# v three tiles ahead of k, and two LN1 transposes moved from TensorE to DMA, in a fused linear-attention and GEGLU kernel

## The chip, the cores and the metric

The kernel runs on one core of one Trainium2 chip. Its time is the device time of one execution in microseconds (us); the figure to compare is the median over several runs. One execution was also recorded by the hardware profiler, and every span, wait and duration below comes from that trace. The engines are named as the profile names them: PE is TensorE (with PEld, its weight loads), DVE is VectorE, ACT is ScalarE, POOL is GpSimd, and SP is SyncE, which here only issues DMAs. Each engine executes its own list of instructions in order and meets the others at semaphores.

## The reference

One sequence of S = 2048 rows with D = 640 columns, in bf16, goes through two blocks, both with a residual connection:

```python
def A(x):                       # H = 32 heads of Dh = 20
    qkv = (x @ wqkv) -> q, k, v per head
    pq, pk = q @ w_phi[h], k @ w_phi[h]
    phi_q = concat(softmax(pq), softmax(-pq))     # over the 20 features, so 40 per head
    phi_k = concat(softmax(pk), softmax(-pk))
    kv, z = phi_k^T v, sum over rows of phi_k     # per head: 40 x 20, and 40
    o = (phi_q @ kv) / (phi_q @ z + 1e-6)
    return o @ wo
def B(x):
    return (gelu(x @ w_gate) * (x @ w_up)) @ w_down     # F = 1536
h  = x + A(layernorm(x))
h2 = h + B(layernorm(h))
```

The attention is linear: all of kv must be summed over all rows before any row of o can be made.

## The kernel before

The rows are held as 16 tiles of 128 rows (x_sb, four tiles to a block). What matters here is the first phase, in which every row tile is normalized (LN1), transposed into LN1T, and multiplied by W_v and by a folded W_k.

*Order of work.* The program is written under a manual schedule: each engine executes its instructions in the order in which the Python code emits them. So the code's order is the queue order of every engine, SyncE's DMA queue included.

*Start.* Rows of x and W_v are loaded (lines 183 to 192); W_k is loaded transposed by five DMA transposes (`load_T`, L197). Meanwhile `warm` (L220) runs matmuls on constants. Tiles 0 and 1 are centred only and transposed on TensorE; their scale is applied later, when v and k are read out of PSUM.

*Fold.* `fold` (L224) multiplies the transposed W_k by a block-diagonal form of w_phi (BD), so that k and its feature map take one product, `Wk2`. It goes in five row chunks d = 0 to 4 of 128 rows: six matmuls each into a PSUM tile `wa`, and then one copy (cast) into Wk2, on ScalarE for the d in KA and on VectorE for the others (L249, L251).

*LN1.* `ln_st` emits the statistics of a tile: `bn_stats` and `bn_aggr` on VectorE (L116, L120), then on GpSimd the root (`ve`, `rstd`, L134 and L135), and, where ScalarE applies the norm, `mr` (L140). `ln_ap` applies it, on VectorE (`ln_dve`, L151) or on ScalarE (`ln_act`, L146). The result is transposed into LN1T either by TensorE (five transposes into PSUM, L159, and a copy out, L160) or by a DMA transpose issued by SyncE (L162). Before the change, tiles 2 to 5 go over TensorE and tiles 6 to 15 by DMA.

*v and k.* `v_mm` and `k_tile` are ten matmuls of 128x320 each (L287): five chunks c of LN1T by two halves u. `v_ev` copies v out of PSUM to vS on ScalarE (L307). `k_tile` goes on with two exponentials on ScalarE, of +k and -k (L320), which gives E.

*The passes.* The loop `for t in range(NT)` (L465) has 16 passes. Pass t emits, in this order: LN1 of tile t+6 on ScalarE (L470, from t = 1 on; in pass 4 later in the pass); `k_tile(t)`; in some passes a fold of W_q (FQ) or the products k^T v of finished tiles (`kv_tile`, in the passes that KVG names); `v_mm(t + 4)` and `v_ev(t + 4)`; statistics of later tiles (ST); `k_norm(t)`, which sums E per head on VectorE (L327), takes the reciprocal (L331) and scales v to `vt` on GpSimd and VectorE (L335); and DMA transposes of W_q. So v runs four tiles ahead of k. Tiles 0 to 4 of v are made before the loop.

*PSUM.* In this phase all products go through one pool, `psG`, of four buffers with two banks each (`gtile`, L106). A buffer is free for its next user when the engine that reads it has finished: for v after `v_ev`, for k after both exponentials.

*Later.* At the end of the loop the first q products, their exponentials and the last k^T v follow, W_g, W_u and W_d are loaded (L518, L533 to L536, each behind a small GpSimd copy that holds the load back), and the attention output, second LayerNorm and the GEGLU block are woven together (L688 to L829). `attn_a` (L580) reads the products of phi_q and kv out of PSUM in two copies, one for each half u.

Of the kernel before, what the change touches and what calls it, by code (L numbers as in the profile page):

```python
# [17 lines left out]
def kernel(  # L18
# [12 lines left out]
    nc = tc.nc  # L31
    P = 128
# [5 lines left out]
    NT = S // P  # L38
    NB = NT // 4
    NC = D // P  # L40
# [6 lines left out]
    VP = (0, 2, 4, 6, 9, 11, 12)  # L47
    KA, QA = (0, 1, 2, 4), (0, 1, 2, 3, 4)
    LQ = (7, 8, 9, 9, 10)
# [5 lines left out]

    KVG = {5: (0, 1), 9: (2, 3, 4, 5), 13: (6, 7, 8, 9)}
    KVQ = {0: (10, 11, 12)}
# [48 lines left out]
    def gtile(name):  # L106
        return psG.tile([P, 2, 512], F32, name=name, tag="G")
# [110 lines left out]
    def warm(*cols):  # L218
        for n in cols:
            nc.tensor.matmul(wu[:, 0, 0:n], lhsT=ones[:, 0:P], rhs=ones[:, 0:n], start=True, stop=True)  # L220

    warm(*[512] * 5, 256, *[P] * 14)

# [60 lines left out]

    def proj(ps, t, W, us=(0, 1), rows=False):
        for u, c in sorted(((u, c) for u in us for c in range(NC)), key=lambda x: x[::-1] if rows else x):
            nc.tensor.matmul(ps[:, u, 0:HD], lhsT=lnT(t, c), rhs=W[:, c, u * HD:(u + 1) * HD],  # L287
                             start=(c == 0), stop=(c == NC - 1))
# [3 lines left out]
    def v_mm(t, us=(0, 1)):  # L292
        if 0 in us:
            pv[t] = gtile("pv")
        proj(pv[t], t, Wv, us)
# [15 lines left out]
    def v_tile(t):  # L311
        v_mm(t)
        v_ev(t)

    def k_tile(t):
        pk = gtile("pk")
        proj(pk, t, Wk2, rows=t == 0)
        Ek[t] = ev.tile([P, 2, D], BF16, name="E", bufs=8)
        for s in range(2):
            nc.scalar.activation(Ek[t][:, s, :].rearrange("p (u f) -> p u f", u=2), pk[:, :, 0:HD],  # L320
                                 ACTF.Exp, scale=((lnp[t][2], nrstd[t]) if t in CT else (1.0, -1.0))[s])
# [121 lines left out]
    nc.sync.dma_start(x_sb[1][:, 2:4, :], x_v[:, 6:8, :])  # L443
    nc.sync.dma_start(x_sb[2], x_v[:, 8:12, :])
    nc.sync.dma_start(x_sb[3], x_v[:, 12:16, :])
    fold(WkT, Wk2, False, (0,))
    v_ev(2)
    fold(WkT, Wk2, False, (1,))
    v_mm(3)
    v_ev(3)  # L450
    ln_st(5, act=False, between=lambda: ln_ap(4, on_pe=True))
    fold(WkT, Wk2, False, (2,))
    ln_tp(4, True)
    fold(WkT, Wk2, False, (3, 4))
    v_mm(4)
    ln_ap(5, on_pe=True)
    v_ev(4)
    ln_tp(5)
    ln_st(6)
# [5 lines left out]
    for t in range(NT):  # L465
# [12 lines left out]
        for j in range(len(QT)):  # L478
            if t == QT[j]:
                q_mm(j)  # L480
                q_exp(j)
                for i in KVQ.get(j, ()):
                    kv_tile(i)
        if 0 < t < NT - 4:
            v_mm(t + 4)
        if late:
            ln_ap(t + 6, on_act=True)
        if 0 < t < NT - 4:
            v_ev(t + 4)
        for i in ST.get(t, ()):  # L490
# [26 lines left out]
    nc.gpsimd.tensor_copy(Wg[:, 0, 0:1], Eq[q - 2][:, 0, 1, 0:1])  # L517
    nc.sync.dma_start(Wg, wg_v)  # L518
    for t in range(13, NT):
# [11 lines left out]
    def load_late(j):  # L531

        nc.gpsimd.tensor_copy(Wu[:, 0, 0:1], Eq[j][:, 0, 1, 0:1])  # L533
        nc.sync.dma_start(Wu, wu_v)
        for f in (0, NF // 2):
            nc.sync.dma_start(Wd[:, f:f + NF // 2], wd_v[:, f:f + NF // 2])  # L536

# [42 lines left out]
    def attn_a(t, dve=0):  # L580
        attn_a_mm(t)
        AB, ab = ABs[t % 2], st[t, "ab"]
        for u in ((1, 0) if t in (4,) else (0, 1)):
            (nc.vector.tensor_copy if u >= 2 - dve else nc.scalar.copy)(
                AB[:, :, u * UH:(u + 1) * UH].rearrange("p s (r h) f -> p r s (h f)", r=2),
                ab[u][:, :, 0:2 * QH * KC].rearrange("p r (s x) -> p r s x", s=2))
        st[t] = AB
# [273 lines left out]
```

## Time and profile before

| | us |
|---|---|
| runs shown: median (lowest to highest of 3) | 275.06 (274.69 to 275.68) |
| the profiled execution | 274.73 |
| its span in the trace | 273.0 |
| first matmul of v starts | 6.63 |
| W_k folds and v of tiles 3 and 4 | 11.27 to 16.24 |
| k of tile 0 starts | 16.52 |
| k of tile 3 starts | 23.31 |
| first k^T v | 30.19 |

In the rows of a timeline the first number is the start of a piece of work from the start of the span, the second its length, then engine, line, operation, tiles written and read, shape, and how many instructions were merged. In brackets stands the idle time of the engine just before it and what ended that. TensorE's matmuls overlap at their ends, so the cost of a piece is best read from its start to the start of the next one. A line of the waits has who waited for whom, the total in us, how often, and the longest. The row PEclk has the granted TensorE clock in tenths in 40 equal slices of the span.

### The profile page before, as it was taken

How to read it: one execution, taken by the hardware profiler on the slowest of the kernel's cores; microseconds unless marked ns; L12 is line 12 of the kernel's file. 1: busy time of each engine (PE TensorE's matmuls, PEld its weight loads, DVE VectorE, ACT ScalarE, POOL GpSimd, SP SyncE). 2: the span in 40 equal slices, each digit the busy share in tenths (PEclk: the TensorE clock that was granted, in tenths of full speed). 3: DMA queues.
4: the chain of work that ended last, by engine and by line, in shares of the span. 5: the costliest groups of instructions: out<-in, count | busy, mean ns of one | idle time of the engine just before them, and what ended most of it. 6: DMA issues, size and time to landing. Idle time of an engine off the chain costs nothing.

```text
span 273.0 us, 7260 instructions
## 1 busy us (share of the span) xinstructions
PE 269.2 (99%) x3000; PEld 172.8 (63%) x3000; DVE 174.0 (64%) x331; ACT 140.4 (51%) x241; POOL 101.4 (37%) x221
## 2 busy tenths in 40 slices
PE   8999999999999999999999999999999999999996
PEld 5777777765555887788755455675555576444574
DVE  5889999996675866685457974346778333333332
ACT  5779996887799765364624256213345600223100
POOL 4248988786101226374213464102156400000000
PEclk9999999999999999999999999999999999999999
DMA  7972666351698022323202124110222211000011
GB/s 193 210 252 51 73 77 101 69 114 38 229 361 280 4 50 50 75 59 66 48 26 52 24 51 71 48 50 2 50 48 50 49 48 50 24 0 0 2 48 48
DMA packets 42400, 21.46 MB, mean 79 GB/s; under 512 B 35200, under 2 KB 40576, under 8 KB 42368
## 3 DMA queue, kind: packets, MB, share of 16 engines
q1 hardware_dynamic: 41712, 20.98, 31.7%
q8 instruction: 23, 0.38, 0.6%
q10 hardware_dynamic: 656, 0.03, 0.2%
q14 instruction: 9, 0.07, 0.1%
HBM read 10.18 MB, written 2.62 MB: 47 GB/s over the span
## 4 chain that ended last, share of the span: by engine, by line
PE 95%; DMA 2%; ACT 1%; DVE 1%; SPq 0%; issue 0%
PE gu L697 38%; PE pd L716 19%; PE pq L376 8%; PE po L637 8%; PE pk L287 8%; PE pv L287 7%; PE ab L565 2%; PE kvp L354 2%; DMA Wv<-in_A_wqkv_dram 2%; PE wa L240 1%; PE tp L159 1%; PE pv L303 1%; ACT vS L307 1%; DVE LN1T L160 0%; SPq L187 0%
## 5 line engine op out<-in xcount | busy, mean ns | idle before, releaser
L700 ACT ACTIVATE g<-gu 128x512 bf16<-128x512 f32 (+1 forms) x60 | 30.6, 511 | 63.4 <-PE gu L697 62.5
L703 DVE TENSOR_TENSOR GT<-gu,g 128x512 bf16<-128x512 f32 (+1 forms) x60 | 34.3, 578 | 43.8 <-PE gu L697 31.1
L697 PE MATMUL gu<-LN2T,Wg 128*128 128x512 bf16 (+1 forms) x300 | 61.8, 337 | 0.0
L697 PE MATMUL gu<-LN2T,Wu 128*128 128x512 bf16 (+1 forms) x300 | 61.7, 336 | 0.0
L716 PE MATMUL pd<-Wd,GT 128*128 128x320 bf16 (+2 forms) x396 | 53.5, 295 | 0.0
L716 PEld LDWEIGHTS <-GT 128*128 128x128 bf16 x396 | 37.9, 98 | 14.6 <-DVE GT L703 0.2
L697 PEld LDWEIGHTS <-Wu 128*128 128x128 bf16 x300 | 29.4, 98 | 22.6
L697 PEld LDWEIGHTS <-Wg 128*128 128x128 bf16 x300 | 28.6, 98 | 20.3
L287 PEld LDWEIGHTS <-LN1T 128*128 128x128 bf16 x290 | 27.8, 98 | 10.5
L335 POOL TENSOR_TENSOR vt<-vS,rs 128x672 bf16<-128x672 bf16 x23 | 31.0, 1371 | 5.9 <-DVE rs L331 4.0
L719 DVE TENSOR_TENSOR y<-pd,x_sb 128x320 bf16<-128x320 f32 (+2 forms) x29 | 13.9, 481 | 29.4 <-PE pd L716 29.4
L637 PE MATMUL po<-Wo,oT 128*128 128x320 bf16 x160 | 24.4, 299 | 0.0
L287 PE MATMUL pk<-Wk,LN1T 128*128 128x320 bf16 x160 | 24.2, 299 | 0.0
L376 PE MATMUL pq<-LN1T,Wq 128*128 128x512 bf16 x100 | 23.3, 379 | 0.0
L327 DVE TENSOR_REDUCE sk<-E 128x64 f32<-128x1280 bf16 x16 | 22.9, 1433 | 0.0
L381 ACT ACTIVATE Eq<-pq 128x1024 bf16<-128x1024 f32 (+1 forms) x26 | 20.0, 828 | 3.3 <-PE pq L376 3.3
L146 ACT ACTIVATE ln<-x_sb,v,rstd 128x640 bf16<-128x640 bf16 x14 | 12.9, 920 | 14.3 <-POOL v L676 14.2
L637 PEld LDWEIGHTS <-oT 128*128 128x128 bf16 x160 | 15.5, 98 | 7.0 <-ACT oT L160 0.5
L287 PE MATMUL pv<-Wv,LN1T 128*128 128x320 bf16 x130 | 19.8, 299 | 0.0
L320 ACT ACTIVATE E<-pk 128x640 bf16<-128x640 f32 x28 | 18.3, 716 | 2.2 <-PE pk L287 2.2
L614 DVE TENSOR_TENSOR tt<-AB,w 128x1280 bf16<-128x1280 f32 x12 | 17.8, 1487 | 1.0 <-POOL w L607 0.9
L594 POOL TENSOR_TENSOR pr<-AB 128x64 f32<-128x64 f32 x10 | 6.8, 678 | 28.1 <-DVE AB L575 20.7
(115 smaller groups left out, 295.6 us busy)
## 6 DMA issues: line engine op xcount, KB each, us to landing
out_dram<-y SPq DMA_DIRECT2D x15, 160.0 KB, 1.8
Wg<-in_B_w_gate_dram SPq DMA_DIRECT2D x1, 1920.0 KB, 8.8
Wu<-in_B_w_up_dram SPq DMA_DIRECT2D x1, 1920.0 KB, 8.9
Wd<-in_B_w_down_dram SPq DMA_DIRECT2D x2, 960.0 KB, 12.2
x_sb<-in_A_x_dram SPq DMA_DIRECT2D x2, 640.0 KB, 6.2
Wo<-in_A_wo_dram SPq DMA_DIRECT2D x1, 800.0 KB, 5.0
x_sb<-in_A_x_dram SPq DMA_DIRECT2D x4, 160.0 KB, 2.8
Wv<-in_A_wqkv_dram SPq DMA_DIRECT2D x2, 320.0 KB, 4.6
```

Of the source, the lines that this page charges most:

```text
L287: nc.tensor.matmul(ps[:, u, 0:HD], lhsT=lnT(t, c), rhs=W[:, c, u * HD:(u + 1) * HD], start=(c == 0), stop=(c == NC - 1))
L320: nc.scalar.activation(Ek[t][:, s, :].rearrange("p (u f) -> p u f", u=2), pk[:, :, 0:HD], ACTF.Exp, scale=((lnp[t][2], nrstd[t]) if t in C ...
L327: nc.vector.reduce_sum(sk, Ek[t].rearrange("p s (h f) -> p (s h) f", f=Dh), axis=AX.X)
L335: eng.tensor_tensor(vt[:, s], vS[t % 8], rs[:, s * H:(s + 1) * H, None].to_broadcast([P, H, VC]), ALU.mult)
L376: nc.tensor.matmul(pqs[j][:, i, :], lhsT=Wq2[:, kc, c * P:(c + 1) * P], rhs=LN1T[b][:, kc, :], start=(kc == 0), stop=(kc == NC - 1))
L381: nc.scalar.activation(Eq[j][:, :, s, :], pqs[j][:, 0:len(QG[j])], ACTF.Exp, scale=(1.0, -1.0)[s])
L614: nc.vector.tensor_tensor(tt.rearrange("p s (h f) -> p s h f", f=Dh), num, w[:, :, :, None].to_broadcast([P, 2, H, Dh]), ALU.mult)
L637: nc.tensor.matmul(pos[u], lhsT=st[t][:, c, :], rhs=Wo[:, c, u * HD:(u + 1) * HD], start=(c == 0), stop=(c == NC - 1))
L697: nc.tensor.matmul(gu[i][:, 0:n], lhsT=W[:, c, f * P:(f + 1) * P], rhs=LN2T[b][:, c, a0:a1], start=(c == 0), stop=(c == NC - 1))
L700: nc.scalar.activation(g[:, 0:n], gu[0][:, 0:n], ACTF.Gelu_apprx_tanh)
L703: nc.vector.tensor_tensor(st[b, "g", f][:, a0:a1], gu[1][:, 0:n], g[:, 0:n], ALU.mult)
L716: nc.tensor.matmul(ps, lhsT=st[b, "g", f][:, tl * P:(tl + 1) * P], rhs=Wd[:, f, f0:f1], start=(f == 0), stop=(f == NF - 1))
```

## The change

- The loop makes v three tiles ahead of k, `v_mm(t + 3)`, and tile 4 of v moves from before the loop into pass 1. The first k^T v (tiles 0 and 1) moves from pass 5 to pass 6.
- LN1 of tiles 4 and 5 is transposed by DMA, as that of the later tiles is; the TensorE transposes and the copies out of PSUM for them are gone.
- Before the loop the folds stand in another order, and k of tiles 0 and 1 is begun there by row chunks of W_k: chunks 0 to 2 of tile 0 and chunk 0 of tile 1 before the last fold, chunks 1 to 3 of tile 1 and 3 of tile 0 after it. `k_tile` adds the last chunk. The fold of chunk 2 is copied out by VectorE in place of ScalarE.
- The load of x_sb 2 is cut in two; its second half and x_sb 3 are issued after the DMA transposes of tiles 4 and 5.
- The loads of W_g and W_u are cut in three each, that of W_d in three in place of two.
- The warm-up matmuls have other sizes, with the same columns in all. In `attn_a`, tile 2 in place of tile 4 has its second half copied first.

```diff
-    KA, QA = (0, 1, 2, 4), (0, 1, 2, 3, 4)
+    KA, QA = (0, 1, 4), (0, 1, 2, 3, 4)
-    KVG = {5: (0, 1), 9: (2, 3, 4, 5), 13: (6, 7, 8, 9)}
+    KVG = {6: (0, 1), 9: (2, 3, 4, 5), 13: (6, 7, 8, 9)}
-    warm(*[512] * 5, 256, *[P] * 14)
+    warm(*[512] * 2, *[P] * 28)
-    def proj(ps, t, W, us=(0, 1), rows=False):
-        for u, c in sorted(((u, c) for u in us for c in range(NC)), key=lambda x: x[::-1] if rows else x):
+    def proj(ps, t, W, us=(0, 1), cs=None):
+        order = [(u, c) for u in us for c in range(NC)] if cs is None else [(u, c) for c in cs for u in us]
+        for u, c in order:
+    pks = {}
+
+    def k_part(t, *cs):
+        if 0 in cs:
+            pks[t] = gtile("pk")
+        proj(pks[t], t, Wk2, cs=cs)
+
     def k_tile(t):
-        pk = gtile("pk")
-        proj(pk, t, Wk2, rows=t == 0)
+        if t in pks:
+            pk = pks[t]
+            k_part(t, NC - 1)
+        else:
+            pk = gtile("pk")
+            proj(pk, t, Wk2)
...
     nc.sync.dma_start(x_sb[1][:, 2:4, :], x_v[:, 6:8, :])
-    nc.sync.dma_start(x_sb[2], x_v[:, 8:12, :])
-    nc.sync.dma_start(x_sb[3], x_v[:, 12:16, :])
+    nc.sync.dma_start(x_sb[2][:, 0:2, :], x_v[:, 8:10, :])
     fold(WkT, Wk2, False, (0,))
     v_ev(2)
     fold(WkT, Wk2, False, (1,))
+    ln_st(5, act=False, between=lambda: ln_ap(4))
+    fold(WkT, Wk2, False, (2,))
     v_mm(3)
     v_ev(3)
-    ln_st(5, act=False, between=lambda: ln_ap(4, on_pe=True))
-    fold(WkT, Wk2, False, (2,))
-    ln_tp(4, True)
-    fold(WkT, Wk2, False, (3, 4))
-    v_mm(4)
-    ln_ap(5, on_pe=True)
-    v_ev(4)
-    ln_tp(5)
+    fold(WkT, Wk2, False, (3,))
+    k_part(0, 0, 1, 2)
+    k_part(1, 0)
+    fold(WkT, Wk2, False, (4,))
+    k_part(1, 1, 2)
+    k_part(0, 3)
+    k_part(1, 3)
+    ln_ap(5)
+    nc.sync.dma_start(x_sb[2][:, 2:4, :], x_v[:, 10:12, :])
+    nc.sync.dma_start(x_sb[3], x_v[:, 12:16, :])
     ln_st(6)
     ln_st(7)
...
-        if 0 < t < NT - 4:
-            v_mm(t + 4)
+        if 0 < t < NT - 3:
+            v_mm(t + 3)
         if late:
             ln_ap(t + 6, on_act=True)
-        if 0 < t < NT - 4:
-            v_ev(t + 4)
+        if 0 < t < NT - 3:
+            v_ev(t + 3)
...
-    nc.sync.dma_start(Wg, wg_v)
+    for a, b in ((0, 2), (2, 4), (4, NC)):
+        nc.sync.dma_start(Wg[:, a:b], wg_v[:, a:b])
...
-        nc.sync.dma_start(Wu, wu_v)
-        for f in (0, NF // 2):
-            nc.sync.dma_start(Wd[:, f:f + NF // 2], wd_v[:, f:f + NF // 2])
+        for a, b in ((0, 2), (2, 4), (4, NC)):
+            nc.sync.dma_start(Wu[:, a:b], wu_v[:, a:b])
+        for f in range(0, NF, 4):
+            nc.sync.dma_start(Wd[:, f:f + 4], wd_v[:, f:f + 4])
...
-        for u in ((1, 0) if t in (4,) else (0, 1)):
+        for u in ((1, 0) if t == 2 else (0, 1)):
```

## The prediction

> **What bounds the kernel now.** I read the page's busy shares first, then what TensorE waits for, then its timeline, then ScalarE's, GpSimd's and SyncE's beside it.
>
> ```profile
> PE 269.2 (99%) x3000; PEld 172.8 (63%) x3000; DVE 174.0 (64%) x331; ACT 140.4 (51%) x241; POOL 101.4 (37%) x221
> PEclk9999999999999999999999999999999999999999
> ```
>
> ```profile
> PE wu L220 <- PEq L845: 0.8, 1, 0.8
> PE pv L303 <- DMA Wv<-in_A_wqkv_dram: 0.2, 1, 0.2
> ```
>
> TensorE is busy 99% of 273.0 us at the full granted clock, and its whole list of waits is two lines, both before 6.7 us. "Busy" alone proves little, because matmul ends are modelled; but ten 128x320 matmuls start 1.36 us apart in the whole first half (23.31 to 24.67, say), so there is no hidden idle time. What can be won is work that TensorE no longer does, or the little it loses between 6.6 and 17 us. The TensorE timeline there:
>
> ```profile
> 13.53 0.48 PE L240 MATMUL wa<-BD,WkT 128*128 128x140 bf16 x6
> 13.84 0.44 PE L159 MATMUL tp<-ident,ln 128*128 128x128 bf16 x5
> 14.12 0.84 PE L240 MATMUL wa<-BD,WkT 128*128 128x140 bf16 x12
> 14.87 1.53 PE L287 MATMUL pv<-Wv,LN1T 128*128 128x320 bf16 x10
> 16.24 0.44 PE L159 MATMUL tp<-ident,ln 128*128 128x128 bf16 x5
> 16.52 2.88 PE L287 MATMUL pk<-Wk,LN1T 128*128 128x320 bf16 x20
> ```
>
> Read start to start: five transposes cost 0.28 us (13.84 to 14.12, 16.24 to 16.52), one fold 0.31 (13.53 to 13.84), two folds 0.75 (14.12 to 14.87), so about 0.13 us there is waiting.
>
> ScalarE in the same stretch, then VectorE and GpSimd, which feed it:
>
> ```profile
> 18.08 0.79 ACT L320 ACTIVATE E<-pk,rstdc 128x640 bf16<-128x640 f32 x1 [0.35 <-PE pk L287]
> 18.77 0.79 ACT L320 ACTIVATE E<-pk,nrstd 128x640 bf16<-128x640 f32 x1
> 19.82 0.92 ACT L146 ACTIVATE ln<-x_sb,mr,rstd 128x640 bf16<-128x640 bf16 x1 [0.26 <-POOL mr L140]
> 20.65 0.77 ACT L320 ACTIVATE E<-pk,va 128x640 bf16<-128x640 f32 x1
> 21.32 0.78 ACT L320 ACTIVATE E<-pk,nrstd 128x640 bf16<-128x640 f32 x1
> ```
> ```profile
> 15.46 0.44 DVE L151 TENSOR_SCALAR ln<-x_sb,mv,rstd 128x640 bf16<-128x640 bf16 x1
> 15.81 0.88 DVE L116 BATCH_NORM_STATS2 stats<-x_sb 128x6 f32<-128x320 bf16 x2
> ```
> ```profile
> 18.05 0.43 POOL L140 TENSOR_SCALAR mr<-mv,rstd 128x1 f32<-128x1 f32 x1
> 19.52 0.26 POOL L140 TENSOR_SCALAR mr<-mv,rstd 128x1 f32<-128x1 f32 x1
> ```
>
> The line with 0.26 carries the forecast. ScalarE's LN1 of tile 7 stands ahead of the exponentials of k of tile 1, and already waits for a small GpSimd result that is ready at 19.78. That result comes 3.97 us after VectorE starts the statistics of tile 6 at 15.81, through a serial run of GpSimd instructions that waits for nothing on TensorE.
>
> SyncE issues all transfers in program order, each taking its time there:
>
> ```profile
> 11.65 0.58 SPq L443 DMA_DIRECT2D x_sb<-in_A_x_dram  x1
> 12.28 0.42 SPq L444 DMA_DIRECT2D x_sb<-in_A_x_dram  x1
> 18.46 19.69 SPq L162 DMA_TRANSPOSE LN1T<-ln  x8
> ```
>
> Whatever is put between the second and the third line moves the loads or the transposes behind it.
>
> **The change, part by part.**
>
> *Transposes of tiles 4 and 5.* TensorE loses two groups of 0.28 = 0.56 us. Their copies out of PSUM go too (0.49 on VectorE, 0.69 on ScalarE). The fold evacuation of W_k rows 2 moves from ScalarE (0.70) to VectorE (0.81): VectorE gets 0.32 us more and stood idle 0.19 and 0.69 us just there (before 12.55 and 14.32), so it is hidden; without that cover it would cost 0.32. ScalarE gets 1.4 us less.
>
> *Order to pass 3.* Folds 0 and 1 as before (to 12.17), fold 2 to 12.48, v of tile 3 to 13.9, fold 3 to 14.2, then k parts, fold 4 and k parts. The casts that these wait for end before they are needed: rows 2 on VectorE about 14.4 (wanted 14.7), rows 3 about 15.1 (wanted 16.1), rows 4 on ScalarE about 16.4 (wanted 16.7). So the 0.13 of waiting goes, some 0.04 comes back before v of tile 3, and TensorE is 0.65 us ahead: k of tile 0 ends at 16.96, k of tile 1 at 17.23, v of tile 4 at 18.59. k of tile 3, which started at 23.31 with one more v tile (1.36) done before it, is wanted at 23.31 - 1.36 - 0.65 = 21.30.
>
> *What is late next.* Four double-bank PSUM buffers serve k and v. When k of tile 3 wants one, k1, v4, k2 and v5 hold them, and the first free is that of k1, after both its exponentials. ScalarE reaches those only after LN1 of tile 7, and that only after GpSimd's result. In the new order VectorE starts the statistics of tile 6 no sooner than its own queue allows (about 15.42, after LN1 of tile 5) and no sooner than its rows land (issued at 11.65, 4.0 us to landing: 15.65). So the chain moves forward by 0.13 to 0.39 us, not by 0.65: the exponentials of tile 1, which ended at 21.32 + 0.78 = 22.10, end between 21.71 and 21.97, and k of tile 3 starts 0.04 later. TensorE waits 0.45 to 0.71 us there. With the v tile added back, 21.75 + 1.36 and 22.01 + 1.36 against 23.31: -0.20 to +0.06 us. I take -0.07, the middle, since the landing is the measured bound but less traffic follows behind it. The saving is nearly all given back.
>
> *After pass 3.* ScalarE's pass takes 2.57 us (22.00, 24.57 and 27.13 start its copies of v), TensorE's 2.72, so ScalarE is not late again. VectorE's chain from 20 us on is the same instructions in the same order, and does not hear of TensorE's lead. The first k^T v (tiles 0 and 1) took 0.88 at 30.19, against 1.45/2 = 0.73 each pair at 54.68; in pass 6, at about 31.5, its operands (VectorE's last at 29.87) are long ready: between 0 and 0.15 won, I take 0.10. The second, in pass 9, comes 1.4 us earlier than before (near 40.6), and its tile 5 needs a VectorE product that ends at 41.3; three tiles at 0.42 come first, to 41.9: no cost. By pass 13 all the moved v tiles are made up.
>
> *DMAs.* On SyncE the transpose of tile 4 issues at about 13.05 behind three row loads instead of being TensorE work; issue to landing of such transposes is 2.6 us in an empty queue (the median from 17 us on) and up to 5.1 (the W_k transposes in the full one): 15.7 to 18.2. It is wanted at 17.23, and the wait at k of tile 3 hides it until about 17.7. I take 16.5, as the queue empties by then. Tile 5 (issue 15.55, wanted 19.95) has more room. The rest of x_sb 2 and x_sb 3 goes from 12.28/12.75 to about 16.8/17.25; with the slowest such load (6.8) that is 24.05, and VectorE reads them from 24.13 on: nothing, but the margin is thin. SyncE's five more issues for W_g, W_u and W_d (0.4 each) delay the last by 2 us; W_u landed at 74.78 + 8.9 = 83.7 and is read from 89.7: nothing; SyncE's next transpose is past 94.
>
> *The rest.* The warm-up matmuls keep 4,608 columns, and at 0.107 us per 128 end where they did (4.83); what follows waits for VectorE's operand and then for W_v, landed at 6.6: nothing either way. The order of the two copies of tiles 2 and 4 out of PSUM changes which buffer comes free first, by one copy (0.75 on ScalarE, 0.89 on VectorE) at most in either direction: nothing where no wait stood before.
>
> **Sum.** -0.07 - 0.10 = about -0.2 us (ends: -0.35 and +0.06). The profiled execution is 274.73 us (span 273.0 and 1.7 around it), so 274.5 on its scale; the three runs have 275.06 as median, 0.33 above it, and on that scale I say 274.9. 0.3% (0.83 us) is about what a measurement of this kernel can tell from no change.
>
> **The rivals.**
>
> *The saving is kept.* If VectorE and GpSimd get through the statistics of tiles 6 and 7 much sooner than 15.42 allows, k of tile 3 does not wait: -0.65 - 0.10, 274.3. Against it: VectorE's queue order. Chance 0.14, and 0.06 of it past 0.3%.
>
> *A transposed tile lands late: slower.* Place: v of tile 4. Each us after 17.7 costs one. The load of x_sb 2 took 5.7 us from issue in this very stretch; so long a transpose lands at 18.75, costs 1.0 and makes about 275.9. For it: landings come in order of issue there, and the transpose stands behind loads. Against it: the load before it is now half as long. The same holds for tile 6 behind x_sb 3 (wanted at 23.1 to 23.4). Decides from a landing of 18.6 on. Chance 0.14, 0.09 of it past 0.3%. The Trainium skill (DMA: Bandwidth & Descriptors, Queues, rings and completion order) says that each DMA engine takes the descriptors of one issuing engine's ring in ring order; by that rule the transpose cannot pass the loads, and the trace agrees so far as every landing from 9 to 19.5 us is in order of issue.
>
> *TensorE's clock rises later: slower.* At the start 128 columns take 0.107 us, and from 6.2 us on 0.056. If the altered warm-up moved that point, each us later costs 0.5; a half-rate stretch half as long again as the 5.4 us seen would cost 1.35, so 276.3. Against it: the same columns with no gap between them. Chance 0.05. The Trainium skill (TensorE: Matmul & The Clock Gate, Part 1) says the gate opens after a busy free-running window, a matter of time and not of how many matmuls; by it the change does nothing, and no single trace can show the run-to-run part.
>
> *A later PSUM wait* from the changed rotation of buffers, 0.75 to 0.9 at one place after 88 us: 275.8. Chance 0.09, 0.04 past 0.3%.
>
> **How the numbers follow.** Forecast 0.58, with its own range 274.5 to 275.4 (the ends, and the 0.4 by which the runs shown lie below and above); rivals 0.14, 0.14, 0.05, 0.09. Faster by over 0.3%: 0.06. Slower: 0.09 + 0.05 + 0.04 + 0.02 of the forecast's tail = 0.20. Same: 0.74. The range is 274.2 to 275.9.
>
> **What would show it.** TensorE should list a wait of 0.4 to 0.8 us for ScalarE's exponentials at the start of k of tile 3 (near 21.3), and ScalarE about 1 us for GpSimd before LN1 of tile 7; there are ten transposes fewer on TensorE; tile 4 lands by 17.7; kv in pass 6 takes under 0.85. No such wait, or one for a DMA before v of tile 4, proves me wrong.

## The result, and the profile after

| | before | after |
|---|---|---|
| median (lowest to highest), 22 runs each, us | 275.05 (274.55 to 276.20) | 275.82 (275.31 to 276.83) |
| ratio after / before | | 1.0027 [1.0017, 1.0037] |
| profiled execution, us | 274.73 | 275.34 |
| its span, us | 273.0 | 273.3 |
| time minus span, us | 1.67 to 1.79 (runs of the kernel before beside the experiments) | 2.03 to 2.15 (these 22 runs) |

The change made the kernel slower by 0.27%, some 0.7 us. The forecast had been 0.2 us faster. In the profiled executions the difference is 0.6 us, of which 0.24 lies inside the span and the rest outside it, where the forecast had not looked.

*The start of the passes came out as forecast.* TensorE's waits of the changed kernel:

```profile
PE wu L220 <- PEq L862: 0.8, 1, 0.8
PE pv L304 <- ACT LN1T L160: 0.7, 1, 0.7
PE tp L159 <- DVE xc L264: 0.6, 1, 0.6
PE pk L288 <- ACT E L332: 0.4, 1, 0.4
```

The last line is the foretold wait of k of tile 3 for ScalarE's exponentials. The three above it lie before 6.7 us and move nothing: v starts at 6.66, against 6.63. TensorE's and ScalarE's timelines around the wait:

```profile
18.61 1.52 PE L288 MATMUL pk<-Wk,LN1T 128*128 128x320 bf16 x10
19.97 1.52 PE L288 MATMUL pv<-Wv,LN1T 128*128 128x320 bf16 x10
21.94 1.52 PE L288 MATMUL pk<-Wk,LN1T 128*128 128x320 bf16 x10 [0.45 <-ACT E L332]
```
```profile
19.60 0.92 ACT L146 ACTIVATE ln<-x_sb,mr,rstd 128x640 bf16<-128x640 bf16 x1 [0.94 <-POOL mr L140]
20.43 0.77 ACT L332 ACTIVATE E<-pk,va 128x640 bf16<-128x640 f32 x1
21.10 0.78 ACT L332 ACTIVATE E<-pk,nrstd 128x640 bf16<-128x640 f32 x1
```

ScalarE is idle for 0.94 us before LN1 of tile 7, waiting for GpSimd's `mr`; both exponentials of k of tile 1 stand behind it and end at 21.88, and k of tile 3 starts at 21.94. The saved transposes are given back here: with the v tile added back, 21.94 + 1.36 = 23.30, against 23.31 before. At 32.30, after the first k^T v, TensorE is 0.14 us ahead of where it was before at the same work (32.44).

*What the forecast did not have.* TensorE's timeline around the k^T v of tiles 6 to 9 in pass 13, first before, then after:

```profile
54.68 1.52 PE L354 MATMUL kvp<-vt,E 128*32 128x42 bf16 x160
56.13 1.53 PE L287 MATMUL pk<-Wk,LN1T 128*128 128x320 bf16 x10
```
```profile
54.59 1.84 PE L366 MATMUL kvp<-vt,E 128*32 128x42 bf16 x160
56.36 1.53 PE L288 MATMUL pk<-Wk,LN1T 128*128 128x320 bf16 x10
```

The same 160 matmuls took 1.45 us from start to next start before, and 1.77 after. TensorE enters 0.09 ahead and leaves 0.23 behind, and is 0.24 behind at the end of the span. All operands are there (the last product of tile 9 is ready at 52.2). The extra time is two gaps, 0.13 us from 55.40 and 0.18 us from 56.03, in which matmuls and weight loads stop together with no wait listed. I call such a gap a stumble. Stumbles are not new: in the kernel before, the group of pass 9 has two (0.06 us from 42.50 and 0.14 from 43.16) and takes 1.69 us, and that of pass 5 has one (0.07 from 30.72). New is that pass 13 has them.

*Outside the span.* Time minus span is some 0.35 us longer: no run of the changed kernel is under 2.03, and none of the kernel before over 1.79. In the trace's events the last semaphore update comes 2.27 us after the end of the span in place of 1.91.

So three costs had to be explained: the wait at k of tile 3 (foretold, some 0.45), the k^T v of pass 13 (0.32) and the end (0.35).

### The profile page after: what moved, and what is told of

Its sections match the earlier page's. It is cut to its first block, busy times and chain, and to the rows that moved or that the text cites. A ratio compares the mean times of both kernels' runs of the same rounds, so it can differ in the third digit from the quotient of the medians.

```text
span 273.3 us, 7252 instructions
## 1 busy us (share of the span) xinstructions
PE 267.0 (98%) x2981; PEld 172.2 (63%) x3000; DVE 175.0 (64%) x331; ACT 138.6 (51%) x239; POOL 100.8 (37%) x221
## 4 chain that ended last, share of the span: by engine, by line
PE 92%; ACT 2%; DVE 2%; issue 1%; DMA 1%; POOL 1%; ACTq 0%; POOLq 0%
PE gu L714 38%; PE pd L733 19%; PE po L654 8%; PE pq L388 8%; PE pk L288 7%; PE pv L288 6%; PE ab L582 2%; PE kvp L366 2%; PE wa L240 1%; DMA x_sb<-in_A_x_dram 1%; PE tp L159 1%; PE pv L304 1%; ACT vS L308 1%; ACT E L332 1%; ACT LN1T L160 0%
## 5 line engine op out<-in xcount | busy, mean ns | idle before, releaser
L347 POOL TENSOR_TENSOR vt<-vS,rs 128x672 bf16<-128x672 bf16 x23 | 30.4, 1344 | 7.3 <-DVE rs L343 4.6
L332 ACT ACTIVATE E<-pk 128x640 bf16<-128x640 f32 x28 | 18.9, 760 | 3.3 <-PE pk L288 3.3
```

The costliest lines, as they stand in the source:

```text
L347: eng.tensor_tensor(vt[:, s], vS[t % 8], rs[:, s * H:(s + 1) * H, None].to_broadcast([P, H, VC]), ALU.mult)
```

## The experiments

Eighteen kernels; the table has the medians of each, with the kernel before run on the same chip. "kv 13" is the k^T v group of pass 13, start to next start, in the profiled execution. "Entries" is the number of VectorE's entries in the trace, its semaphore instructions included.

| run | us | before | ratio [95%] | span | outside span | kv 13 | VectorE entries |
|---|---|---|---|---|---|---|---|
| e1_after | 275.43 | 274.78 | 1.0029 [1.0018, 1.0039] | 273.35 | 2.08 | 1.76 | 440 |
| e2_nosplit | 275.78 | 274.78 | 1.0030 [1.0019, 1.0041] | 273.7 | 2.07 | 1.78 | 440 |
| e3_oldwarm | 276.61 | 274.78 | 1.0063 [1.0046, 1.0080] | 274.5 | 2.11 | 1.76 | 440 |
| e4_ln7late | 275.02 | 274.78 | 1.0008 [0.9999, 1.0016] | 272.9 | 2.11 | 1.78 | 440 |
| e5_before_newwarm | 277.21 | 274.86 | 1.0079 [1.0052, 1.0106] | 275.5 | 1.72 | 1.46 | 441 |
| e6_pad_act | 275.09 | 274.86 | 0.9999 [0.9987, 1.0011] | 273.0 | 2.09 | 1.78 | 440 |
| e7_pad_pool | 275.11 | 274.86 | 0.9996 [0.9978, 1.0015] | 273.05 | 2.10 | 1.76 | 440 |
| e8_pad_dve | 274.86 | 274.86 | 0.9996 [0.9978, 1.0014] | 273.15 | 1.73 | 1.62 | 464 |
| e9_one_dve | 274.96 | 274.76 | 0.9999 [0.9985, 1.0012] | 273.25 | 1.72 | 1.76 | 441 |
| e10_before_less | 275.25 | 274.76 | 1.0011 [0.9996, 1.0026] | 273.2 | 2.08 | 1.46 | 440 |
| e11_kv5 | 275.51 | 274.76 | 1.0036 [1.0021, 1.0051] | 273.75 | 1.73 | 1.63 | 441 |
| e12_best | 274.63 | 274.76 | 0.9991 [0.9982, 1.0001] | 272.9 | 1.72 | 1.77 | 441 |
| e13_before_transpose | 275.29 | 275.0 | 1.0014 [0.9992, 1.0036] | 273.5 | 1.80 | 1.77 | 442 |
| e14_before_load | 274.87 | 275.0 | one run | 273.1 | 1.77 | 1.46 | 442 |
| e15_best_moved | 275.32 | 275.0 | 1.0018 [1.0003, 1.0032] | 273.2 | 2.10 | 1.77 | 440 |
| e16_window_free | 274.94 | 274.83 | 0.9991 [0.9975, 1.0008] | 273.05 | 1.88 | 1.76 | 444 |
| e17_before_issues | 275.46 | 274.8 | 1.0019 [1.0006, 1.0033] | 273.65 | 1.81 | 1.46 | 442 |
| e18_queue_idle | 278.98 | 274.8 | 1.0146 [1.0116, 1.0175] | 277.0 | 1.98 | 1.47 | 443 |

The ratios weigh the runs against their neighbours and differ from the quotient of the medians by up to 0.0013 (e7, e16), so a difference of 0.3 us between two medians says little by itself; time minus span, which is nearly the same in all runs of a kernel, says more. The waits and timelines shown are those of one profiled execution of each kernel, which can lie anywhere among its runs. The last row of a view can be cut off by the view's window.

### The changed kernel again, without the splits, and with the old warm-up

The first is the changed kernel itself. The second and third undo one part each:

```diff
-    for a, b in ((0, 2), (2, 4), (4, NC)):
-        nc.sync.dma_start(Wg[:, a:b], wg_v[:, a:b])
+    nc.sync.dma_start(Wg, wg_v)
...
```
```diff
-    warm(*[512] * 2, *[P] * 28)
+    warm(*[512] * 5, 256, *[P] * 14)
```

> The changed kernel once more, whole. Theory A (the loss is spread: TensorE's saving is given back in the wait at k of tile 3, TensorE then loses about 0.3 us more inside two dense groups of k^T v, and about 0.3 us lies outside the span): the wait of 0.4 to 0.5 us at k of tile 3 and the two interruptions in pass 13 come back, the span is 0.2 to 0.4 us longer than that of the kernel before, the time 0.6 to 0.9 us longer. Rival B (the profiled execution was an odd one): the interruptions in k^T v do not come back and the span is equal.

> The changed kernel with W_g, W_u and W_d loaded in the old pieces (five DMAs fewer). Theory A says that the splits have nothing to do with TensorE: the same time as the changed kernel within 0.1 us inside the span. Rival C (the extra DMAs cost time at the end or start of the program, outside the span): 0.3 us shorter, with the span unchanged.

> The changed kernel with the old warm-up matmuls (ten instructions fewer ahead of everything on TensorE, of weight loads as well). Theory A as I hold it gives no effect at the start: v starts at 6.6 to 6.7 us either way. If the interruptions in the dense k^T v groups hang on where these groups stand in TensorE's instruction stream, moving the stream by 20 instructions moves or removes them: up to 0.3 us either way. Rival D (the smaller matmuls delay the full clock): 0.3 to 0.7 us faster with the old ones, and the clock's rise earlier.

Measured again, the loss is the same, 0.29%, half of it (0.35) outside the span; the wait and the slow k^T v are there again. Without the splits the ratio is 1.0030, against 1.0029: they are worth nothing that these runs can tell, as forecast.

The old warm-up was not neutral: 1.2 us slower than the changed kernel. The waits with it, in an execution that was the slowest of its six (277.42):

```profile
PE pv L288 <- DMA LN1T<-ln: 1.7, 1, 1.7
PE pk L288 <- ACT E L332: 0.7, 1, 0.7
```

The transposed tile 4 now lands at 19.00, not 17.02, and v of tile 4 waits for it: the forecast's rival "a transposed tile lands late", at the foretold place. What moved it is seen in the DMA view from 12 to 15.8 us (queue, packets, MB, share of 16 engines), first the changed kernel, then this one:

```profile
q8 instruction: 1, 0.02, 1.5%
```
```profile
q8 instruction: 1, 0.02, 4.5%
```

The one 16 KB packet of TensorE's instructions took 2.71 us here (4.5% of 16 engines over 3.8 us) and 0.94 there, and the rows issued just before tile 4's transpose landed 2 us later, at 17.56. That the packet held up the rows is argued from the order in time, not shown. The median of the six is only 1.2 us above the changed kernel, so the executions did not all lose as much.

### LN1 of tile 7 behind the exponentials of k of tile 1

```diff
-        late = t == 4
+        late = t in (1, 4)
```

> The changed kernel with LN1 of tile 7 emitted on ScalarE behind the exponentials of k of tile 1 instead of ahead of them. Theory A: the wait of 0.45 us at k of tile 3 goes, and with nothing else late TensorE stays 0.45 us ahead to the end of the span, so 0.4 to 0.5 us faster than the changed kernel. Rival E (another resource, VectorE's or GpSimd's chain to k^T v, bounds the phase): the wait turns up again at k^T v of pass 9 or 13 and the time stays within 0.1 us.

The wait at k of tile 3 is gone; of TensorE's waits one is left, at the start, and k of tile 3 follows v without a gap:

```profile
PE wu L220 <- PEq L862: 0.8, 1, 0.8
```
```profile
20.18 1.52 PE L288 MATMUL pv<-Wv,LN1T 128*128 128x320 bf16 x10
21.54 1.52 PE L288 MATMUL pk<-Wk,LN1T 128*128 128x320 bf16 x10
```

The median is 0.41 us below that of the changed kernel beside it, for a wait of 0.45, and so is the median span, by 0.45. That is the mechanism of the forecast, shown by removing it. What remains against before is the end (2.11 outside the span).

### The new warm-up in the kernel before

> The kernel before with only the warm-up sizes of the changed kernel (20 more TensorE instructions ahead of the rest). The old warm-up put back into the changed kernel cost 1.2 us, with TensorE's second block of instructions fetched at 13.05 for 2.7 us in place of 12.9 for 0.9, and the transpose of tile 4 landing at 19.0. Theory F (the warm-up sizes set when that fetch falls among the row loads and transposes): here the fetch moves from 14.6 to about 13, and the time stays within 0.2 us of the kernel before, because no transposed tile is waited for there; if the fetch hits W_k's transposes, W_k's last rows land after 14.4 and up to 0.5 us is lost. Rival D (the sizes matter through the clock): 0.3 us faster or more.

Only the warm-up line of the change was made, which is ten matmuls and ten weight loads more with the same columns. I expected next to nothing; it cost 2.35 us. TensorE's waits, in the fastest of its four executions (276.34):

```profile
PE pq L376 <- issue: 1.0, 1, 1.0
PE wa L240 <- ACT Wk L249: 0.4, 1, 0.4
```

One gap of a microsecond in q, in which TensorE waits for nothing that the profile shows, and a late fold (its W_k chunk landed at 14.98, not 13.69). So either warm-up costs 1.2 to 2.4 us when put with the other order of work. These two waits explain most of the 1.6 us by which this execution is above the profiled one of before; the further 0.9 us up to the median is in no trace. Why a list of TensorE's instructions that is shifted by twenty brings such waits is not shown.

### The end: 24 idle instructions on each engine, then one

```diff
+    pad = const.tile([P, 1], F32, name="pad")
...
     def gate_up(b, f, a0, a1):
+        if b >= 2:
+            nc.vector.memset(pad, 0.0)
```

This is the kernel with LN1 of tile 7 later (e4), with 24 one-column writes that nobody reads, on ScalarE, GpSimd and VectorE in turn (shown: VectorE).

> LN1 of tile 7 late, and 24 copies of one column added on ScalarE, one ahead of each gate and up product of the last two blocks, where ScalarE is mostly idle. The time outside the span is 1.73 us in every run of the kernel before and 2.0 to 2.1 in every run of the changed kernel and its variants. Theory G (one engine's instruction stream ends at an unlucky place for the fetch of its last instructions, and the end of the program waits for it): if the engine is ScalarE, the part outside falls back to 1.7. Rival H (it hangs on the number of DMAs or on something else): it stays at 2.1. Span: unchanged within 0.1.

> The same with 24 one-column memsets on GpSimd in place of ScalarE's copies. Theory G, if the engine is GpSimd: 1.7 us outside the span in place of 2.1. Otherwise 2.1. Span: unchanged within 0.1.

> The same with 24 one-column memsets on VectorE. Theory G, if the engine is VectorE: 1.7 us outside the span in place of 2.1. Otherwise 2.1. Span: unchanged within 0.1.

ScalarE's and GpSimd's leave 2.1 us outside the span; VectorE's give 1.73 again. In the execution with VectorE's another transposed tile was late: tile 6, whose transpose stands behind the load of x_sb 3 in SyncE's queue. (The writes come long after, and e4, whose instructions are the same up to there, has no such wait: the landing varies from one execution to the next.)

```profile
23.49 1.53 PE L289 MATMUL pv<-Wv,LN1T 128*128 128x320 bf16 x10 [0.55 <-DMA LN1T<-ln]
```

The Trainium skill (DMA: Bandwidth & Descriptors, Queues, rings and completion order) says that each DMA engine consumes its ring in order, though not that transfers complete in that order. Here they did: in the changed kernel the transposes of tiles 4 and 5, the two row loads and the transpose of tile 6 land in the order of their issue, at 17.02, 18.21, 20.58, 22.29 and 22.98.

VectorE's list is one entry shorter in the changed kernel than before (440 and 441), so the next two runs ask for one instruction: one more in the changed kernel, and one fewer in the kernel before.

```diff
+        if (b, f) == (3, 0):
+            nc.vector.memset(pad, 0.0)
```
```diff
-        nc.vector.memset(vS[i][:, :, Dh], 1.0)
+        (nc.gpsimd if i == 7 else nc.vector).memset(vS[i][:, :, Dh], 1.0)
```

> The changed kernel with one more VectorE instruction (one memset of a column that nobody reads, in the GEGLU block of row block 3). Theory G (the 0.35 us between time and span hangs on VectorE's list being one instruction shorter than before): time minus span 1.70 to 1.79 in every run, span as in the changed kernel (273.3), time 275.1, 0.3 less than the changed kernel's 275.4. Rival (24 memsets took it away by their number or place, one is not enough): time minus span 2.0 to 2.13, 275.4.

> The kernel before with one VectorE instruction fewer: one of the eight memsets of ones at the start goes to GpSimd. Theory G: time minus span goes from 1.73 to 2.0 to 2.13, with nothing else of the change made; the span stays within 0.2 us, so the time is 0.3 us above before. Rival (the last step of the closing barrier goes with something else of the change, and the 24 memsets hit it by chance): time minus span stays 1.70 to 1.79 and the time is before's.

Both came out, as theory G has it: 1.68 to 1.78 us in every run of the changed kernel with one instruction more, 2.05 to 2.11 in every run of the kernel before with one fewer, which has nothing else of the change. A later run with 440 entries (e15, where a moved instruction dropped a semaphore entry) had 2.04 to 2.15. Why 440 entries end slower than 441 is not shown, and it is no simple step: kernels with 443 and 444 have 1.76 to 2.1.

### The first k^T v back in pass 5

```diff
-    KVG = {6: (0, 1), 9: (2, 3, 4, 5), 13: (6, 7, 8, 9)}
+    KVG = {5: (0, 1), 9: (2, 3, 4, 5), 13: (6, 7, 8, 9)}
```

> The kernel of the run with one more VectorE instruction, and the first k^T v back in pass 5. Theory K (moving the first k^T v is what makes the later groups of k^T v stumble): the groups of passes 9 and 13 take 1.69 and 1.45 us without interruptions in the second, and TensorE is 0.2 to 0.3 us ahead of the run with the memset alone from 57 us on. Rival (the stumble belongs to the order of v and k): the group of pass 13 takes 1.7 to 1.8 us as in the changed kernel, and the time is within 0.15 us.

0.55 us slower than the kernel of e9 that it was made from. TensorE's timeline shows where 0.41 of it goes: in the new order pass 5 comes too early for VectorE.

```profile
28.73 0.47 PE L367 MATMUL kvp<-vt,E 128*32 128x42 bf16 x40
29.62 0.47 PE L367 MATMUL kvp<-vt,E 128*32 128x42 bf16 x40 [0.41 <-DVE vt L348]
```

Tile 1's product is late. The move to pass 6 belongs to the shift of v, then. Pass 13 still stumbles (1.63, not 1.46), so theory K falls, though the rival's 1.7 to 1.8 did not come either.

### The two known costs removed

```diff
-        late = t == 4
+        late = t in (1, 4)
...
     ln_st(5, act=False, between=lambda: ln_ap(4))
+    nc.sync.dma_start(x_sb[2][:, 2:4, :], x_v[:, 10:12, :])
...
     ln_ap(5)
-    nc.sync.dma_start(x_sb[2][:, 2:4, :], x_v[:, 10:12, :])
-    nc.sync.dma_start(x_sb[3], x_v[:, 12:16, :])
+    nc.sync.dma_start(x_sb[3][:, 0:2, :], x_v[:, 12:14, :])
...
             ln_ap(6)
+            nc.sync.dma_start(x_sb[3][:, 2:4, :], x_v[:, 14:16, :])
...
+        if (b, f) == (3, 0):
+            nc.vector.memset(pad, 0.0)
```

> The changed kernel with three things more: LN1 of tile 7 behind the exponentials of k of tile 1 on ScalarE, one more VectorE instruction, and the row loads in another order (second half of x_sb 2 right after the transpose of tile 4, first half of x_sb 3 after that of tile 5, second half of x_sb 3 after that of tile 6). Theory A with G (the wait at k of tile 3 and the 0.35 us outside the span are the two removable costs): no wait of TensorE for ScalarE's exponentials or for a transposed tile over 0.2 us after 17 us, span 272.5 to 272.8, outside 1.7 to 1.8, 274.3 to 274.6, which is 0.1 to 0.2% below before. Rival (transposes land late whatever stands around them): a wait of 0.3 to 0.7 us at v of tile 4 or 6, 274.9.

274.63, against 274.76: the lowest median of the study, at a ratio of 0.9991 whose interval [0.9982, 1.0001] still reaches 1, so not surely faster than before. TensorE's waits all lie before 7 us:

```profile
PE tp L160 <- DVE xc L265: 0.9, 1, 0.9
PE wu L221 <- PEq L866: 0.8, 1, 0.8
PE pv L305 <- DMA Wv<-in_A_wqkv_dram: 0.2, 1, 0.2
```

Its k^T v of pass 13 still takes 1.77, and the median span is 272.9, where the forecast had 272.5 to 272.8.

### The stumbles of pass 13

All kernels with the new order so far had 1.62 to 1.78, all with the old 1.46. In the traces the group with stumbles had the small packets of a DMA transpose in its time (some 430 in the changed kernel; under 20 before). So I put a DMA transpose there in the kernel before, and a plain load of the same bytes:

```diff
             transpose_to(LN1T[0][:, :, P:2 * P], ln_a(1), False)
+            nc.sync.dma_start_transpose(dum, A_wqkv[0:P, 0:D])
```
```diff
             transpose_to(LN1T[0][:, :, P:2 * P], ln_a(1), False)
+            nc.sync.dma_start(dum.rearrange("p c n -> p (c n)"), A_wqkv[0:P, 0:D])
```

> The kernel before with one DMA transpose more: right after that of tile 1 (issued at 52.6), 128 rows of w_qkv go transposed into a tile that nobody reads. Its small packets fall into the k^T v of pass 13 (54.68 to 56.13). Theory T (dense k^T v groups stumble while a DMA transpose's packets are under way): that group takes 1.65 to 1.8 us in place of 1.46, with one or two interruptions of 0.1 to 0.2 us, and the groups of passes 5 and 9 stay as they were (0.87, 1.69). Rival S (the stumble belongs to the order of TensorE's instructions): 1.46.

> The same with a plain load of the same 160 KB in place of the transpose. Theory T in its narrow form (it is the transpose's small packets): the group of pass 13 takes 1.46. In its wide form (any transfer under way does it): 1.6 to 1.8. Rival S: 1.46.

SyncE's and TensorE's timelines, first with the transpose, then with the load:

```profile
53.72 1.21 SPq L163 DMA_TRANSPOSE LN1T<-ln  x1
54.97 1.28 SPq L497 DMA_TRANSPOSE dum<-in_A_wqkv_dram  x1
```
```profile
55.27 1.84 PE L355 MATMUL kvp<-vt,E 128*32 128x42 bf16 x160
57.04 1.12 PE L288 MATMUL pk<-Wk,LN1T 128*128 128x320 bf16 x7
```
```profile
53.80 0.58 SPq L497 DMA_DIRECT2D dum<-in_A_wqkv_dram  x1
55.39 1.88 SPq L163 DMA_TRANSPOSE LN1T<-ln  x1
```
```profile
54.59 1.53 PE L355 MATMUL kvp<-vt,E 128*32 128x42 bf16 x160
56.05 1.12 PE L288 MATMUL pk<-Wk,LN1T 128*128 128x320 bf16 x7
```

1.77 against 1.46, in one profiled execution of each: with a transpose the old order stumbles as the new one does, with a load it does not. (By time, e13 cannot be told from before: 1.0014 [0.9992, 1.0036].) The packets themselves do not fit, though. In the changed kernel the first gap, 55.40 to 55.52, has no DMA packet in it or in the 0.5 us before it, as nearly all of the transpose's packets come after 55.8. Next I tried to take the transposes out of the window in the new order: LN1 of tiles 1 and 0 earlier, and then the copies of kmask out of their way.

```diff
-        if t == 10:
+        if t == 9:
             transpose_to(LN1T[0][:, :, P:2 * P], ln_a(1), False)
-        if t == 12:
+        if t == 10:
             ln_ap(0, on_act=True)
```
```diff
-        if t == 9:
+        if t == 11:
             for r in (1, 2, 3):
                 nc.sync.dma_start(kmask[QUAD[r]], kmask[QUAD[0]])
-        if t == 11:
+        if t == 13:
             nc.gpsimd.tensor_copy(KV[:, 0, :, KC - 1], kmask)
```

> The kernel of the last run (LN1 of tile 7 later, one VectorE instruction more, row loads in another order) with the second normalization and DMA transpose of tiles 1 and 0 moved from passes 10 and 12 to 9 and 10, so that both have landed by about 54. Theory T: the k^T v of pass 13 takes 1.46 to 1.5 in place of 1.77, span 272.5 to 272.7, 274.2 to 274.4, 0.13 to 0.2% below before. Rival S: the group stays at 1.77, 274.6. Against both: if ScalarE or VectorE, which do that work 3 to 5 us earlier, now hold a k product back, there is a wait of TensorE of 0.2 to 0.5 us near 46 to 50.

> The kernel of the last run with the three small copies of kmask moved from pass 9 to pass 11 on SyncE's queue (their reader on GpSimd from pass 11 to 13), so that the transposes of tiles 1 and 0 issue by about 51 and have landed by about 54, and with four VectorE memsets in place of one. Theory T (a DMA transpose's packets make the k^T v group stumble): under 150 small packets in the window of that group, and it takes 1.46 to 1.5 us in place of 1.77; span 272.5 to 272.7. Rival S (order of TensorE's instructions): 1.77 whatever the packets. Theory G: VectorE has more than 440 entries again, so time minus span 1.7 to 1.8. Both together: 274.2 to 274.4, some 0.2% below before.

The first moved nothing that counts: SyncE came to tile 0's transpose no sooner, at 54.48, in the midst of the group (53.91 to 55.68). The second did clear the transposes, as SyncE's timeline shows, but the group still took 1.76:

```profile
52.37 1.22 SPq L163 DMA_TRANSPOSE LN1T<-ln  x1
53.69 1.87 SPq L527 DMA_DIRECT2D kmask<-kmask  x3
55.60 0.59 SPq L532 DMA_DIRECT2D Wo<-in_A_wo_dram  x1
```
```profile
54.37 1.83 PE L367 MATMUL kvp<-vt,E 128*32 128x42 bf16 x160
56.13 1.12 PE L289 MATMUL pk<-Wk,LN1T 128*128 128x320 bf16 x7
```

Only 53 small packets fall into its first quarter of a microsecond, and some 100 after that, about as many as the copies of kmask have rows. So theory T, that a transpose's packets do it, does not hold as it stood. What all slow groups still shared was that SyncE was issuing DMAs in their first 0.8 us. The last two runs put three small plain loads there in the kernel before, and meant to leave SyncE idle there in the new order (kmask in passes 8 and 11).

> The kernel before with three small plain loads (128 rows of 256 bytes each, into a tile that nobody reads) in place of the one plain load, at the same place in SyncE's queue: they issue from 53.8 to 55.6, so SyncE is issuing DMAs in the first 0.8 us of the k^T v group of pass 13 (54.6), where it stood idle before. Theory I (a dense k^T v group stumbles when SyncE issues DMAs in its first 0.8 us, of whatever kind): 1.65 to 1.78 us in place of 1.46. Theory T (the small packets of a DMA transpose do it): 1.46.

> The kernel of the last run with the three copies of kmask moved ahead on SyncE's queue (pass 8; their reader on GpSimd back in pass 11), so that the transposes of tiles 1 and 0 and the load of W_o are all issued by about 54.3 and SyncE is idle in the first 1.2 us of the k^T v group of pass 13. Theory I: that group takes 1.46 to 1.5 us in place of 1.76, span 272.5 to 272.7, 274.2 to 274.5. Theory T: 1.46 too, if the transposes have landed by 54.9. Rival S (order of TensorE's instructions): 1.76.

With the plain loads:

```profile
54.10 1.53 SPq L498 DMA_DIRECT2D dum<-in_A_wqkv_dram  x3
55.73 2.07 SPq L163 DMA_TRANSPOSE LN1T<-ln  x1
```
```profile
54.88 1.53 PE L355 MATMUL kvp<-vt,E 128*32 128x42 bf16 x160
56.34 1.53 PE L288 MATMUL pk<-Wk,LN1T 128*128 128x320 bf16 x10
```

SyncE issues from 54.10 to 55.63 and the group takes 1.46: theory I falls, as issuing plain loads does nothing. The other run came out otherwise than meant, as SyncE now stood waiting for kmask and the transposes of W_q came late:

```profile
PE wa L241 <- DMA WqT<-in_A_wqkv_dram: 3.2, 1, 3.2
```
```profile
58.50 1.54 PE L367 MATMUL kvp<-vt,E 128*32 128x42 bf16 x160
59.97 1.26 PE L289 MATMUL pk<-Wk,LN1T 128*128 128x320 bf16 x8
```

It lost 4 us there. Still, it tells something: the group took 1.47 in the new order of TensorE's instructions, with some 670 small packets in its first microsecond. Neither the order alone nor the packets alone make the stumbles.

*What the traces show together.* I take all gaps of 0.05 us or more in the k^T v groups of passes 5 or 6, 9 and 13, in all twenty traces (before, after and the eighteen), leaving out the one that waits for an operand in e11. Of these 72 gaps 68 begin 0.72 to 0.92 or 1.37 to 1.61 us after SyncE *starts to issue* a DMA transpose, whatever its packets do. The other way round, wherever such a gap is due (0.78 and 1.45 us after the issue's start) later than 0.35 us into a group, there is one within 0.16 us of that; the gaps that would be due in a group's first 0.35 us stay away. For the transpose of tile 0, SyncE's and ScalarE's timelines before:

```profile
54.51 0.94 ACT L146 ACTIVATE ln<-x_sb,mrc,rstdc 128x640 bf16<-128x640 bf16 x1
55.48 2.27 SPq L162 DMA_TRANSPOSE LN1T<-ln  x1
```

and after:

```profile
53.66 0.94 ACT L146 ACTIVATE ln<-x_sb,mrc,rstdc 128x640 bf16<-128x640 bf16 x1
54.62 1.20 SPq L162 DMA_TRANSPOSE LN1T<-ln  x1
```

Pass 13 in all kernels, in us from the start of its group:

| kernels | the nearest transpose's issue starts | gaps start |
|---|---|---|
| before, e5, e10, e14, e17 | 0.80 to 0.85 | none |
| after, e1 to e4, e6, e7, e9, e12 | 0.03 to 0.05 | 0.80 to 0.84, 1.42 to 1.46 (and 1.55 in e12) |
| e8, e11 | 0.04 | 0.83, 0.84 |
| e13 | -0.30 (the added one) | 0.59, 1.17 |
| e15 | -0.81, 0.57 | 0.75, 1.30 |
| e16 | none after -2.00; kmask copies at -0.68, -0.02, 0.60 | 0.83, 1.41 |
| e18 | -1.17 | none |

Before, a gap 0.72 us or more after the issue's start would come at 1.5 us, behind the group's last matmuls; after, both come inside the group. That earlier issue is the change's own doing. With v three tiles ahead, k of tile 12 stands ahead of v of tile 15 on TensorE, its exponentials start at 51.31 in place of 52.76, and LN1 of tile 0, behind them on ScalarE, ends at 54.60 in place of 55.45; the transpose is issued right behind it.

What stays open: what stops TensorE then. The match is read from traces; e13, with one transpose more as its only change, bears it out, but no run moved the transpose of tile 0 alone. In e16 the copies of kmask, which are no transposes, stand 0.8 us ahead of both gaps, while plain loads at such distances (e17) do nothing; and the first group of e13 has a gap of 0.29 us from 30.71 with no transpose issued in the 1.8 us before. The group of e18 is no clean case, as TensorE had stood still for 3.2 us a little earlier. As matmuls and weight loads stop together with no semaphore between, a shortage of instructions would fit. That is an argument, and no run here shows it. The Trainium skill (Runtime: NRT & Kernel Launch, Instruction fetch mechanics) says that instructions come in blocks of 16 KiB through DMA, and that crossing from one block to the next is mostly hidden. The traces agree on the block (23 packets of 16,384 bytes for some 6,000 entries of TensorE, 0.9 to 1.7 us each, once 2.7). None of these packets is under way in a stumble of pass 13: in the changed kernel the next starts at 56.90, behind the group. Whether the crossing is hidden in a group of 320 entries in 1.45 us, the traces do not decide.

## Why the prediction was wrong

*Right, with its sizes.* The wait at k of tile 3 (forecast 0.45 to 0.71 at 21.75 to 22.01; 0.45 at 21.94), its cause (LN1 of tile 7 on ScalarE, waiting for GpSimd; 0.94 idle), and its worth (0.41 when removed). After it the lead is 0.01 us, for a forecast of 0.07 (from -0.06 to 0.20). Tile 4 landed at 17.02, before 17.7. The splits of the late loads are worth nothing.

*Right by luck: the first k^T v.* It took 0.76 in place of 0.87, 0.11 won against 0.10, and so at 32.30 the lead is 0.14 us for a forecast of 0.2. But the forecast put that down to operands, and before they were ready too (29.87, for a start at 30.19). The 0.87 holds a stumble of 0.07 us, which is absent after; in the new order e6 and e16 have one there as well and take 0.91 and 0.92, and e5 in the old order has none and takes 0.76.

*Wrong, first step: "the second, in pass 9 ...: no cost. By pass 13 all the moved v tiles are made up."* I asked only whether the operands are there. They are, and the group of pass 9 took 1.73 in place of 1.69; but that of pass 13 took 1.77 in place of 1.45, 0.32 us, and with it the lead was gone. The sum had no term for it. What the runs show in its place is that a dense group has a price of its own, 1.45 or 1.77 us, with all operands there, and that it goes with when SyncE issues a DMA transpose; why is open. The rows of before had a hint that I passed over: I took 0.42 a tile in pass 9 and 0.73 a pair in pass 13 for the same work, and 0.88 for the pair at 30.19 as a matter of operands, though no wait was listed there.

*Wrong, second step: "span 273.0 and 1.7 around it".* I carried the 1.7 over as a constant. It went to 2.08, as VectorE has one entry fewer (e9 and e10). The sum had no term for it and no rival covered it. Without these 0.35 us the change could not be told from before (e9: 0.9999 [0.9985, 1.0012]).

*Wrong, without weight in the sum: the warm-up "nothing either way".* In the changed kernel the old warm-up costs 1.2 us and in the kernel before the new one 2.35. The columns are the same, but TensorE's instruction list is not.

*Of the rivals,* "the saving is kept" fell. "A transposed tile lands late" did not happen in the changed kernel, but it is close: it came with the old warm-up (1.7 us), and, once the wait at k of tile 3 was gone, at tile 6 in e8 (0.55), though not in e4. "TensorE's clock rises later" did not happen: in the profiled execution a 128-column matmul takes 0.107 us until 3.6 us and 0.06 from there, where before the half rate lasted until 6.2. No later PSUM wait was listed.

So the step that failed in sign is the sum's end. Measured, the change stands at -0.14 us at 32 us, -0.09 by 54.6 and +0.23 behind the group of pass 13, and some 0.35 come on top outside the span. The median of 275.82 lies within the stated range of 274.2 to 275.9, but for none of the reasons that the forecast gave for slower.

## What to carry to other kernels

A saving on the bounding engine is worth nothing where the next buffer's release hangs on another engine's queue order: look there first, as moving one instruction (LN1 of tile 7) gave 0.4 us here, out of the 0.65 that the edit had saved on TensorE up to there. When the question is a few tenths of a percent, take the time outside the span and the unlisted gaps inside dense groups as terms of their own, and read them in every run. An edit that "only" changes how many instructions an engine has was not free here: test it by itself. And where a shift on one engine makes another finish sooner, look at what that one triggers: here a transpose came to be issued at the start of a dense group.

## What the runs showed of the hardware that I had not expected

- One VectorE instruction more or fewer moved the time outside the span between 1.73 and 2.08 us, in every run and in both directions. In two kernels with 443 and 444 entries, where it was 1.76 to 2.1, an instruction packet of 8,192 bytes appears behind the end of the span (at 274.9 us where the span ends at 273.2, and at 278.8 where it ends at 277.0).
- Ten warm-up matmuls more, with the same columns, made the kernel before 2.35 us slower. In the profiled execution a gap of 1.0 us at 63.5, far from the warm-up, has no semaphore behind it.
- A dense group of 160 short matmuls had gaps 0.72 to 0.92 and 1.37 to 1.61 us after SyncE started to issue a DMA transpose (68 of 72 gaps in twenty traces). One transpose added in the kernel before made it 1.77 us in place of 1.46; a plain load of the same size, or three smaller ones, left it at 1.46 (one profiled execution each).
